# The z1 half of a gMLP input projection by a seven-product block algorithm

## The chip, the cores and the metric

The kernel runs on one NeuronCore of one Trainium2 chip. The metric is the device time of one execution in microseconds, as the median of several runs. Beside the timed runs, one further execution was recorded by the hardware profiler; all views below are of that execution.

The engines are named as the profile names them: PE is TensorE (PEld its weight loads), DVE is VectorE, ACT is ScalarE, POOL is GpSimd, SP is SyncE, which here only issues DMAs.

## The reference, cut to what matters

```python
S, D, F = 2048, 1024, 3584; Fh = F // 2            # bf16 in, bf16 out
h  = x + attention(layernorm(x))                   # 32 heads, 4 segments of 512 tokens
# the part that the change touches, with x = layernorm(h):
z  = gelu(x @ w_in)                                # w_in: 1024 x 3584
z1 = z[:, :Fh]                                     # 2048 tokens x 1792
z2 = layernorm(z[:, Fh:])
g  = w_sp @ z2 + b_sp[:, None]                     # w_sp: 2048 x 2048, over tokens
h2 = h + (z1 * g) @ w_out                          # w_out: 1792 x 1024
```

`gelu` is the tanh approximation.

## The kernel before, in words

Every operation is first recorded by a small recorder (`_Recorder.record`), which finds for each operation the earlier ones on other engines, or in DMA queues, that it has to wait for, by the memory cells that both touch. `emit` then writes each engine's operations out in the recorded order, so that all instructions carry one line in the profile, L210. The order of the program text is thus the order in each engine's own queue: an operation that waits holds up everything recorded after it on the same engine. On SP the same holds for DMA issues. SBUF regions are assigned by hand (`tens(name, shape, type, offset)`), and many are used by several tensors in turn.

The work runs in these stages, with the times of the profiled execution:

- **Attention**, to about 289 us, segment by segment, with the projections and the out-projection (`wo`) filled in between. Its last part puts the normalised activations into `HNT[s]`, four tensors of 128 x 8 x 512 bf16: for each segment s the 1024 features on partitions (eight blocks of 128) and 512 tokens along the row.
- **z2**, to 405 us: `z2_group(k, tc)` (line 798) multiplies one chunk of 128 tokens with 448 columns of `w_in`, eight matmuls into one PSUM bank, and ACT takes the bank with gelu into `Z2`. For each of four column chunks k (loaded by `win_load`, line 792, into `WIN`) it runs over 16 token chunks. `z2_stats` collects mean and variance on DVE, POOL makes the reciprocal deviation (`ZRS`), and `z2_apply` (line 822) writes the normalised chunk as fp16 into `Z2H`, on DVE, 128 x 1792. Between the groups ACT also squares the 16 row blocks of `w_sp` (`sp_norm`, line 916), because `sp_scale` (line 919) derives from the sum of squares a power of two, `SC`, with which `w_sp` is scaled to fp16.
- **z1**, to 501.5 us: the loop at line 1073 goes over four segments and 14 column blocks of 128. Each makes eight matmuls of 128 x 512, over the eight feature blocks, with the weights in `WIZ`, and ACT writes gelu into `Z1T` (features on partitions, 14 blocks, 2048 tokens). In the same stage SP loads blocks of `w_sp` transposed (`sp_load`, line 966), DVE scales them to fp16 (`sp_half`, line 971) and makes their block sums (`sp_sum`, line 974: `t1` to `t4`) and the first sums of z2 (`s_sum`, line 981, into the four parts of `SS`).
- **The gate**, `gate_group` (line 1001), in two periods (`pr`), each for 1024 output tokens. `g = w_sp @ z2` is already computed by an algorithm that cuts both factors into 2 x 2 blocks and needs seven block products instead of eight, with sums of blocks as factors (Strassen's, in Winograd's form). A group of columns has seven products (`prod`, line 991), each of eight fp16 matmuls of 128 x 512 into one bank. ACT copies the first product (`tmp_s1`), POOL adds two rows of `b_sp` (`BROW`) to it, DVE adds up the banks (`stt`), multiplies with `Z1T` in place (`out`) and makes the next group's `SS`.
- **Out**: after each period 16 units of 14 matmuls with `w_out` (`out_unit`, line 1054), added to h on DVE and stored. Next period's `w_sp` blocks are loaded and scaled meanwhile.

PSUM has eight banks, taken in rotation by `next_bank`.

Of the kernel before, what the change touches and what calls it, by code (L numbers as in the profile page):

```python
# [258 lines left out]
def bass_sequential_preLN__memory_aug_infini_attn__mixer_gmlp__prompt_kernel(  # L259
# [31 lines left out]
    class Bump:  # L291
# [4 lines left out]
        def __call__(self, name, shape, dt):  # L296
# [63 lines left out]
    WIN = [tens("win%d" % i, [128, 8, 512], BF16, o * K) for i, o in enumerate((46, 54, 190))]  # L360
    WIZ = [tens("wiz%d" % i, [128, 8, w], BF16, o * K)
           for i, (o, w) in enumerate(((54, 512), (190, 512), (118, 512), (126, 256)))]
# [3 lines left out]
    ROLES = (("b11", 46), ("b12", 22), ("b21", 198), ("b22", 14))  # L366
    RAW = {k: tens(k + "r", [128, 8, L], BF16, o * K) for k, o in ROLES}
    BH = {k: tens(k + "h", [128, 8, L], F16, o * K)
          for k, o in ROLES + (("t1", 30), ("t2", 190), ("t3", 22), ("t4", 38))}
    SS = tens("ss", [128, 4, 8, 128], F16, 54 * K)  # L370
# [3 lines left out]
    ZRS = b3("zrs", [128, NTC], F32)  # L374
    ONES = b3("ones", [128, 128], BF16)
    MHZ = b3("mhz", [128, 1], F32)
    SQ = b3("sq", [128, 16], F32)
    SQB = b3("sqb", [128, 16], BF16)
    TOT = b3("tot", [128, 1], F32)
    TOP = b3("top", [128, 1], F32)  # L380
    SC = b3("sc", [128, 1], F32)
    INV = b3("inv", [128, 1], F32)
# [3 lines left out]
    BROW = [tens("brow%d" % i, [128, L], BF16, (132 + i) * K) for i in range(2)]  # L386
    WO0 = tens("w_out0", [128, 14, 512], BF16, 118 * K)
    WO1A = tens("w_out1a", [128, 7, 512], BF16, 54 * K)
    WO1B = tens("w_out1b", [128, 7, 512], BF16, 4 * K)
    FIN = [tens("fin%d" % i, [128, 512], BF16, o * K) for i, o in enumerate((61, 11, 12, 13))]  # L390
# [26 lines left out]
    def wcols(ap, lo, hi):  # L417
        return ap[:, lo:hi].rearrange("(c p) n -> p c n", p=128)
# [371 lines left out]
    CH = [("z2", FH + 448 * k, 448) for k in range(4)] + [("z1", 512 * k, min(512, FH - 512 * k)) for k in range(4)]  # L790

    def win_load(k):
        kind, lo, w = CH[k]
        sp.dma_start((WIN[k % 3] if k < 4 else WIZ[k - 4])[:, :, 0:w], wcols(B_w_in, lo, lo + w))

    zs, zq, staged = [], [], []

    def z2_group(k, tc, stage=None):
        s, tcl = divmod(tc, 4)
        b = next_bank()  # L800
        wi = WIN[k % 3]
        mm8(PS[:, b, 0:448], lambda i: HNT[s][:, i, tcl * 128:(tcl + 1) * 128], lambda i: wi[:, i, 0:448])
        if stage is None:
            z2_gelu(k, tc, PS[:, b, 0:448])
        else:
            act.activation(ZSTG[stage][:], PS[:, b, 0:448], ACTF.Copy)
            staged.append((k, tc, ZSTG[stage][:]))
# [5 lines left out]
    def z2_stats():  # L813
        k, tc = zs.pop(0)
        dve.bn_stats(ZST[:, tc, k, :], Z2[:, tc, k * 448:(k + 1) * 448])
        if k == 3:
            dve.bn_aggr(ZMV[:, tc, :], ZST[:, tc, :, :])
            pool.tensor_single_scalar(ZRS[:, tc:tc + 1], ZMV[:, tc, 1:2], float(LN_EPS), ALU.add)
            pool.tensor_tensor(ZRS[:, tc:tc + 1], ZRS[:, tc:tc + 1], MHALF[:], ALU.pow)
            zq.append(tc)  # L820

    def z2_apply():
        tc = zq.pop(0)
        dve.tensor_scalar(Z2H[:, tc, :], Z2[:, tc, :], ZMV[:, tc, 0:1], ZRS[:, tc:tc + 1], ALU.subtract, ALU.mult)

# [93 lines left out]
    def sp_scale(b):  # L919
        pe.matmul(PS[:, b, 0:16], ONES[:], SQB[:], start=True, stop=True)  # L920
        dve.tensor_reduce(out=TOT[:], in_=PS[:, b, 0:16], axis=mybir.AxisListType.X, op=ALU.add)
        dve.tensor_single_scalar(TOT[:], TOT[:], 1e-30, ALU.max)
        pool.tensor_tensor(TOP[:], TOT[:], MHZ[:], ALU.pow)
        dve.tensor_single_scalar(TOP[:].bitcast(I32), TOP[:].bitcast(I32), 0x7F800000, ALU.bitwise_and)
        dve.tensor_single_scalar(SC[:], TOP[:], 8192.0, ALU.mult)
        dve.reciprocal(INV[:], SC[:])

# [3 lines left out]
    for it in todo:  # L931
        if isinstance(it, int):
            for half in range(2):
                wo(NSEG - 1, it, half)
                bg_pop()
            continue
        z2_group(*it)
        if it == (0, 12):
            sp_norm_load(0)
            sp_norm_load(1)  # L940
        if it[0] and it[1] > 3 or it[0] > 1:
            q = 16 * it[0] + it[1] - 20
            r = (q * 16 + 15) // 44
            if r < 16 and (q * 16 - 1) // 44 < r:
                sp_norm(r)
                if r < 14:
                    sp_norm_load(r + 2)
                elif r == 15:
                    pool.tensor_copy(SQB[:], SQ[:])
        bg_pop()  # L950
        z2_stats()
        if len(zs) > 1:
            z2_stats()
        if len(zq) > 1:
            z2_apply()
        if it == (0, NTC - 1):
            win_load(3)
        if it == (1, NTC - 1):
            for k in (4, 6, 7):
                win_load(k)  # L960
        if it == (2, NTC - 1):
            win_load(5)
# [8 lines left out]
    def sp_half(k):  # L971
        dve.tensor_single_scalar(BH[k][:], RAW[k][:], SC[:], ALU.mult)

    def sp_sum(o, a, b):
        dve.tensor_tensor(BH[o][:], BH[a][:], BH[b][:], ALU.subtract)
# [25 lines left out]
    def gate_group(pr, g, ba):  # L1001
        t1, t2 = slice(1024 * pr, 1024 * pr + 512), slice(1024 * pr + 512, 1024 * pr + 1024)
        s1, s1b1, s1b2, u2, u3 = (TMP[k][:] for k in ("s1", "s1b1", "s1b2", "u2", "u3"))
        inv = INV[:]
# [10 lines left out]
        pool.tensor_tensor(s1b1, s1, BROW[0][:], ALU.add)  # L1015
        bb, bc = next_bank(), next_bank()
# [3 lines left out]
        if pr == 0 and g == 0:  # L1020
            sp_sum("t4", "b21", "t2")
        if g < 6:
            s_sum(1, g + 1)
        prod(bb, SS[:, 2], "t3", False)
        prod(ba, a_blk(0, 1, g), "b21", False)
# [3 lines left out]
        nb = prod1(g + 1) if g < 6 else None  # L1029
        if g < 6:  # L1030
            s_sum(3, g + 1)
        stt(s1, ba, BROW[0][:])
        out(s1, 0, t1)
        prod(bc, SS[:, 3], "b22", False)
        if g < 6:
            s_sum(2, g + 1)
        prod(bb, a_blk(1, 1, g), "t4", False)
# [4 lines left out]
        stt(s1b1, bb, s1b1)  # L1042
        out(s1b1, 1, t1)
# [25 lines left out]
    for j in range(4):  # L1069
        sp_load(0, "b21", j)  # L1070
    for j in range(4):
        sp_load(0, "b11", j)
    for s in range(NSEG):
        for fc in range(14):
            k, fl = divmod(fc, 4)
            b = next_bank()
            mm8(bank(b), lambda i: WIZ[k][:, i, fl * 128:(fl + 1) * 128], lambda i: HNT[s][:, i, :])
            act.activation(Z1T[:, fc, s * 512:(s + 1) * 512], bank(b), ACTF.Gelu_apprx_tanh)
            if zq:
                z2_apply()  # L1080
            if s == 0 and fc == 6:
                sp_scale(next_bank())
            if s == 2 and fc in (6, 12):
                for k in ("b21", "b11", "b22") if fc == 6 else ("b12",):
                    sp_half(k)
            if s == 3:
                if fc == 0:
                    sp_sum("t1", "b12", "b11")
                if fc == 4:
                    s_sum(1, 0)  # L1090
                    s_sum(2, 0)
                    s_sum(3, 0)
                    s_sum(4, 0)
                if fc == 2:
                    sp_sum("t3", "b22", "b12")
                if fc == 8:
                    sp_sum("t2", "b22", "t1")
        if s == 0:
            for j in range(4):
                sp_load(0, "b22", j)  # L1100
        if s == 1:
            for j in range(4):
                sp_load(0, "b12", j)
            brow_load(0)
    sp.dma_start(WO0[:], wout[:, :, 0:512])

    units = [(tc, 0, 512) for tc in range(6)] + [(tc, 512, 512) for tc in range(8)] + [(tc, 0, 512) for tc in (6, 7)]
    nb = prod1(0)
    for g in range(7):
        nb = gate_group(0, g, nb)  # L1110
# [6 lines left out]
    act.dma_start(WO1A[:], wout[:, 0:7, 512:D])  # L1117
    act.dma_start(WO1B[:], wout[:, 7:14, 512:D])
    for n, u in enumerate(units):
        if n + 2 < 16:  # L1120
            fin_load(units[n + 2], act)
        out_unit(u, (lambda i: WO0[:, i, :]) if u[1] == 0 else
                 (lambda i: WO1A[:, i, :] if i < 7 else WO1B[:, i - 7, :]), act)
        if n == 1:
            sp_half("b11")
        if n == 4:
            sp_half("b12")
            sp_sum("t1", "b12", "b11")
        if n == 6:
            sp_half("b22")  # L1130
            sp_sum("t3", "b22", "b12")
        if n == 8:
            sp_sum("t2", "b22", "t1")
        if n == 10:
            sp_half("b21")
            sp_sum("t4", "b21", "t2")
        if n == 13:
            for k in range(1, 5):
                s_sum(k, 0)
# [9 lines left out]
    for n, u in enumerate(units):  # L1149
        if n + 2 < len(units):  # L1150
            fin_load(units[n + 2])
        tc, lo, w = u
        out_unit(u, (lambda i: WO0[:, i, 0:w]) if lo == 0 else (lambda i: Z1T[:, i, lo - 512:lo - 512 + w]))

# [29 lines left out]
```

## Time and profile before

| | us |
|---|---|
| median of three runs | 771.69 (771.63 to 772.64) |
| the profiled execution, its own time | 772.03 |
| its span, from first to last instruction | 770.3 |
| z2 stage, PE alone at work on `win` and the last `wo` | about 289 to 405.0 |
| z1 stage (`hnT,wiz` matmuls) | 405.0 to 501.5 |
| gate, first period | 501.5 to 586.4 |
| out, first period | 586.4 to 634.5 |

The page of the profile gives first the busy time of each engine and its share of the span, then the same in 40 slices, where a digit is tenths, with the clock that TensorE was granted. Section 4 is the chain of work that ended last, followed backwards from the last instruction. Section 5 groups instructions by line, engine, operation, and written and read tiles, with shapes; "x439 | 96.2, 379" reads: 439 of them, 96.2 us busy, 379 ns each. Matmuls overlap, so 379 ns is the latency of one and not its pace. The timeline shows instructions in order of time, start and length, like ones merged, and in brackets how long the engine had been idle and what ended it.

### The profile page before, as it was taken

Reading aid. Unit: us, or ns where it says so; the run is one execution under the profiler, and the core shown is the slowest. Engines: PE = TensorE matmul, PEld = TensorE weight load, DVE = VectorE, ACT = ScalarE, POOL = GpSimd, SP = SyncE. Lnnn points to the kernel's source line nnn. Section 1 sums busy time; section 2 is a strip of 40 time slices with the busy share of each in tenths; the row PEclk is TensorE's granted clock in tenths of the full one; section 3 lists DMA queues with packets and bytes.
Section 4 is the critical chain, followed back from the end, with each engine's and each line's share of the span. In section 5 each row is a group of like instructions: output and inputs, shape, how many; then the busy total and the mean of one; then the engine's idle time right before and its main releaser. Section 6 shows DMA issues by size and latency. Waiting matters only on the chain.

```text
span 770.3 us, 13128 instructions
## 1 busy us (share of the span) xinstructions
PE 761.2 (99%) x5476; PEld 367.2 (48%) x5551; DVE 464.5 (60%) x846; ACT 334.2 (43%) x395; POOL 200.0 (26%) x361
## 2 busy tenths in 40 slices
PE   8999999999999999999999999999999999999998
PEld 4445555545554545455554444444444444444444
DVE  5586589768964676754366202278785756878422
ACT  6777877777777767157783333310000000000000
POOL 2564556555653333100033000021110002112000
PEclk9999999999999999999999999999999999999999
DMA  9654555364425331765672230020019850000222
GB/s 305 168 152 89 97 83 125 83 97 84 96 57 131 84 83 37 210 173 183 198 219 55 55 67 2 1 96 1 1 34 206 229 169 7 1 1 0 62 83 75
DMA packets 133900, 75.06 MB, mean 97 GB/s; under 512 B 96208, under 2 KB 124624, under 8 KB 133840
## 3 DMA queue, kind: packets, MB, share of 16 engines
q1 hardware_dynamic: 126592, 67.40, 36.0%
q10 hardware_dynamic: 7248, 6.82, 2.8%
q8 instruction: 43, 0.70, 0.4%
q14 instruction: 17, 0.14, 0.1%
HBM read 42.74 MB, written 8.39 MB: 66 GB/s over the span
## 4 chain that ended last, share of the span: by engine, by line
PE 93%; DVE 5%; issue 1%; DMA 1%; ACT 0%; DVEq 0%
PE ps L210 93%; DVE stats L210 1%; DMA wv<-in_A_wv_dram 1%; DVE hch L210 1%; DVE otok L210 0%; DVE pqk L210 0%; DVE lno L210 0%; DVE ta L210 0%; DVE etmp L210 0%; DVE rd L210 0%; DVE rdm L210 0%; DVE mv L210 0%; ACT e L210 0%; ACT L210 0%; DVE upd L210 0%
## 5 line engine op out<-in xcount | busy, mean ns | idle before, releaser
L210 ACT ACTIVATE e<-ps 128x2048 bf16<-128x2048 f32 (+1 forms) x96 | 152.7, 1590 | 41.7 <-PE ps L210 41.5
L210 POOL TENSOR_SCALAR_AFFINE_SELECT e<-e 128x512 bf16<-128x512 bf16 x128 | 90.6, 720 | 132.4 <-ACT e L210 132.3
L210 POOL TENSOR_TENSOR tmp_s1b<-tmp_s,brow 128x512 f32<-128x512 f32 x28 | 32.3, 1155 | 255.1 <-ACT tmp_s L210 223.7
L210 PE MATMUL ps<-win,hnT 128*128 128x448 bf16 x512 | 98.3, 352 | 0.0
L210 PE MATMUL ps<-hnT,wiz 128*128 128x512 bf16 x439 | 96.2, 379 | 0.5
L210 ACT ACTIVATE tmp_s<-ps,inv 128x512 f32<-128x512 f32 x14 | 9.6, 687 | 195.1 <-DVE z1T L210 131.6
L210 PEld LDWEIGHTS ps<-win,hnT 128*128 128x128 bf16 x512 | 49.7, 98 | 46.4 <-issue 0.2
L210 PEld LDWEIGHTS ps<-hnT,wiz 128*128 128x128 bf16 x448 | 43.7, 98 | 52.7
L210 ACT ACTIVATE z1T<-ps 128x512 bf16<-128x512 f32 x56 | 33.4, 597 | 63.3 <-PE ps L210 61.1
L210 PE MATMUL ps<-xnT,wk 128*128 128x512 bf16 x233 | 59.6, 380 | 1.2
L210 PE MATMUL ps<-wv,xnT 128*128 128x512 bf16 x255 | 59.5, 380 | 0.9 <-DMA wv<-in_A_wv_dram 0.5
L210 PE MATMUL ps<-wo,oT 128*128 128x512 bf16 x254 | 57.7, 380 | 0.1
L210 DVE BATCH_NORM_STATS2 zst<-z 128x6 f32<-128x448 bf16 x64 | 38.4, 617 | 31.8 <-ACT z L210 31.3
L210 DVE TENSOR_TENSOR fin<-fin,ps 128x512 bf16<-128x512 bf16 (+2 forms) x33 | 22.1, 671 | 56.6 <-PE ps L210 48.4
L210 PE MATMUL ps<-xnT,wq 128*128 128x512 bf16 x226 | 54.0, 379 | 1.6
L210 PE MATMUL ps<-w_out,z1T 128*128 128x512 bf16 x218 | 49.3, 379 | 0.3
L210 ACT ACTIVATE z<-ps 128x448 bf16<-128x448 f32 x60 | 31.5, 541 | 37.4 <-PE ps L210 37.4
L210 PEld LDWEIGHTS ps<-v,e 128*128 128x128 bf16 x1280 | 38.8, 96 | 14.0 <-issue 6.5
L210 PE MATMUL ps<-v,e 128*128 128x33 bf16 x1280 | 42.2, 178 | 0.0
L210 DVE SCALAR_TENSOR_TENSOR tmp_u<-ps,inv,tmp_s1b 128x512 f32<-128x512 f32 x28 | 21.0, 750 | 31.3 <-PE ps L210 16.7
L210 PEld LDWEIGHTS ps<-wo,oT 128*128 128x128 bf16 x256 | 24.1, 98 | 27.6
L210 PEld LDWEIGHTS ps<-xnT,wk 128*128 128x128 bf16 x256 | 22.6, 98 | 29.9 <-issue 5.0
(137 smaller groups left out, 1101.0 us busy)
## 6 DMA issues: line engine op xcount, KB each, us to landing
sj<-in_B_w_sp_dram SPq DMA_DIRECT2D x16, 512.0 KB, 3.5
xch<-in_A_x_dram SPq DMA_DIRECT2D x16, 256.0 KB, 3.6
xr<-in_A_x_dram SPq DMA_DIRECT2D x16, 256.0 KB, 4.0
out_dram<-hch SPq DMA_DIRECT2D x16, 256.0 KB, 2.4
win<-in_B_w_in_dram SPq DMA_DIRECT2D x4, 896.0 KB, 5.3
wiz<-in_B_w_in_dram SPq DMA_DIRECT2D x3, 1024.0 KB, 6.2
wo<-in_A_wo_dram SPq DMA_DIRECT2D x1, 2048.0 KB, 8.7
fin<-out_dram ACTq DMA_DIRECT2D x16, 128.0 KB, 3.4
```

The source lines that it names most:

```text
L210: ins = getattr(e, op.name)(*op.args, **op.kw)
```

## The change

z1 is computed by the same seven-product algorithm as the gate. Both factors are cut in two along the features (blocks 0 to 3 and 4 to 7) and, respectively, along the columns (first and second 896) and along the tokens (segments 2p and 2p + 1). A group is now one column block of each half and two segments: 7 groups in each of two periods p, 14 in all, of seven products of four matmuls.

- The weights' z1 half is loaded in column pairs (`WZ`, 2 x 256 columns; the last 2 x 128), scaled in place to fp16 (`WZH`) by a power of two from their largest magnitude (`wz_norm`, DVE; `scale_of`, one matmul on PE in the z2 stage), and the gelu's `scale` takes the power back (`INV[1]`).
- Four sums of weight blocks per group (`sz_sum`, 128 x 512 fp16) are made on POOL, four sums of activations per period (`hn_sum`, in halves of 128 x 1024) on DVE.
- In a group ACT copies the first product, DVE adds banks (five operations of 128 x 512), ACT writes four gelus. The products of successive groups are interleaved by the table `offs`.
- `z2_apply` leaves the z2 stage: eight run on DVE and eight on ACT, in z1's first eight groups.
- The fp16 scaling of the first period's `w_sp` blocks moves from DVE to ACT, in quarters (`sp_part`), in z1's groups 8, 9, 10 and 12; their transposed loads move to z1's second half.
- `t1`, `t2` and the first `SS` follow after z1's last step on DVE; `t3` and `t4` are made in the first gate group, half on POOL and half on DVE, in quarters. Ahead of that PE gets the first two products of groups 0 and 1 (`pre`). `brow_load` follows after z1, and `BROW[1]` takes the region of one of the weight sums.
- In `gate_group` the order of some operations changes.
- The squares of `w_sp` are spread over 37 groups of z2 instead of 44, and many regions move.

The core of the diff:

```diff
+    def wz_load(q):
+        w = 256 if q < 3 else 128
+        for i in range(2):
+            lo = 896 * i + 256 * q
+            sp.dma_start(WZ[q][:, :, i, :], wcols(B_w_in, lo, lo + w))
...
+    def hn_sum(p, t, h, eng=dve):
+        a, b = {1: (hb(0, 1, p), hb(0, 0, p)), 2: (hb(1, 1, p), HT[p][1][:]),
+                3: (hb(1, 1, p), hb(0, 1, p)), 4: (hb(1, 0, p), HT[p][2][:])}[t]
+        s = slice(2 * h, 2 * h + 2)
+        eng.tensor_tensor(HT[p][t][:, s, :], a[:, s, :], b[:, s, :], ALU.subtract)
...
+    for r in range(16):
+        q = (37 * r + 15) // 16
+        at(q, sp_norm, r)
+        if r < 14:
+            at(q, sp_norm_load, r + 2)
+    at(37, pool.tensor_copy, SQB[:], SQ[:])
+    for k in range(12):
+        at(k + 1, wz_norm, (1, 2, 0)[k // 4], k % 4)
+    for k in range(8):
+        at(3 + 2 * k, hn_sum, 0, (1, 2, 3, 4)[k // 2], k % 2)
+    at(18, wz_norm, 3, 0)
+    at(19, wz_norm, 3, 1)
+    at(20, pool.tensor_copy, SQB[:, 0:14], SQZ[:])
+    at(25, scale_of, 1, 14, None)
+    for k in range(8):
+        at(26 + k, wz_half, k // 2, k % 2)
...
-        if len(zq) > 1:
+        if len(zq) > 16:
             z2_apply()
         if it == (0, NTC - 1):
+            for k in (1, 2, 0):
+                wz_load(k)
             win_load(3)
...
-    for s in range(NSEG):
-        for fc in range(14):
-            k, fl = divmod(fc, 4)
-            b = next_bank()
-            mm8(bank(b), lambda i: WIZ[k][:, i, fl * 128:(fl + 1) * 128], lambda i: HNT[s][:, i, :])
-            act.activation(Z1T[:, fc, s * 512:(s + 1) * 512], bank(b), ACTF.Gelu_apprx_tanh)
...
+    def z1_step(g, k):
...
+        for i in range(4):
+            pe.matmul(b, ka[:, i, :], kb[:, i, :], start=(first and i == 0), stop=(i == 3), skip_group_check=True)
+        if k == 1:
+            act.activation(s1, b, ACTF.Copy)
+        if k == 6:
+            dve.tensor_tensor(u2, b, s1, ALU.add)
+        if k == 5 and g < 13:
+            for x in (1, 2):
+                sz_sum(g + 1, x)
+        if k == 7:
+            dve.tensor_tensor(u3, b, s1, ALU.add)
+            dve.tensor_tensor(u3, bank(zb[g, 2]), u3, ALU.add)
+            z1_out(fc + 7, 2 * p + 1, u3)
+            if g < 13:
+                sz_sum(g + 1, 3)
+        if k == 2:
+            z1_out(fc, 2 * p, b)
...
+        if k == 4:
+            dve.tensor_tensor(s1, b, s1, ALU.add)
+            z1_out(fc + 7, 2 * p, s1)
+        if k == 3:
+            dve.tensor_tensor(u2, b, u2, ALU.add)
+            z1_out(fc, 2 * p + 1, u2)
+            if g < 12:
+                sz_sum(g + 2, 4)
...
+    for g in range(8):
+        on(g, 6, lambda: zq and z2_apply())
+        on(g, 4, lambda: zq and z2_apply(True))
+    for k in range(8):
+        on((0, 1, 2, 3, 4, 4, 5, 5)[k], 3 if k < 5 else (7, 3, 7)[k - 5], hn_sum, 1, (1, 2, 3, 4)[k // 2], k % 2)
+    on(1, 7, scale_of, 0, 16, None)
+    for k, g, r in (("b11", 6, 3), ("b12", 6, 3), ("b22", 8, 3), ("b21", 10, 3)):
+        for j in range(4):
+            on(g, r, sp_load, 0, k, j)
+    for n, (k, g) in enumerate((("b11", 8), ("b12", 9), ("b22", 10), ("b21", 12))):
+        for r in range(4):
+            on(g, (6, 7, 2, 4)[r], sp_part, k, r)
+    offs = {1: -5, 6: 0, 5: 1, 7: 3, 2: 4, 4: 6, 3: 12}
+    for x, g, k in sorted((7 * g + offs[k], g, k) for g in range(14) for k in offs):
+        z1_step(g, k)
+    for k in ("t1", "t2"):
+        for r in range(4):
+            sp_sum(k, r)
+    for k in range(1, 5):
+        s_sum(k, 0)
+    brow_load(0)
+    for i in range(2):
+        sp.dma_start(WO0[i][:], wout[:, 7 * i:7 * i + 7, 0:512])
...
-    nb = prod1(0)
-    for g in range(7):
+    pre = [(prod1(g), prod2(g)) for g in range(2)]
+    nb2 = gate_group(0, 0, *pre[0])
+    nb = gate_group(0, 1, *pre[1])
+    gate_group(0, 2, nb2, nx=False)
+    for g in range(3, 7):
         nb = gate_group(0, g, nb)
```

And in `gate_group`:

```diff
+        if pr == 0 and g == 0:
+            for r in range(4):
+                sp_sum("t3", r, pool if r < 2 else dve)
         bb, bc = next_bank(), next_bank()
         prod(bb, SS[:, 1], "t2", True)
         prod(bc, SS[:, 0], "t1", True)
         stt(u2, bb, s1b2)
         if pr == 0 and g == 0:
-            sp_sum("t4", "b21", "t2")
+            for r in range(4):
+                sp_sum("t4", r, pool if r < 2 else dve)
+        nb = prod1(g + 1) if bd is None and g < 6 and nx else None
         if g < 6:
             s_sum(1, g + 1)
+            s_sum(2, g + 1)
         prod(bb, SS[:, 2], "t3", False)
-        prod(ba, a_blk(0, 1, g), "b21", False)
+        if bd is None:
+            prod(ba, a_blk(0, 1, g), "b21", False)
+        elif nx:
+            nb = prod1(g + 2)
         stt(u3, bb, s1b2)
```

## The prediction, made before the changed kernel had run

> **What bounds the kernel now.** I read the page's busy shares first, then the chain that ended last, then the timeline of TensorE by stage.
>
> ```profile
> PE 761.2 (99%) x5476; PEld 367.2 (48%) x5551; DVE 464.5 (60%) x846; ACT 334.2 (43%) x395; POOL 200.0 (26%) x361
> PEclk9999999999999999999999999999999999999999
> PE 93%; DVE 5%; issue 1%; DMA 1%; ACT 0%; DVEq 0%
> ```
>
> TensorE is busy 99%, carries 93% of the chain and is at full clock in all 40 slices. From 289 to 768 us the chain is PE with gaps of 0.05 us. Time therefore falls only by removing matmuls, and any wait that newly reaches PE is paid in full. Since PE never waits there, none of the waits costed below can come out under zero.
>
> ```profile
> 405.00 7.29 PE L210 MATMUL ps<-hnT,wiz 128*128 128x512 bf16 x33
> ...
> 501.50 1.89 PE L210 MATMUL ps<-b11h,z2h 128*128 128x512 f16 x8
> 503.23 1.89 PE L210 MATMUL ps<-t2h,ss 128*128 128x512 f16 x8
> ```
>
> z1 runs from 405.00 to 501.50 us: 448 matmuls, 0.2154 us each from start to start. An fp16 product of eight takes 503.23 - 501.50 = 1.73 us, 0.216 each: both types cost the same. (The rows' 379 ns is the latency of one, not its pace.)
>
> **What the change removes.** z1 has 14 groups of 7 products of 4 matmuls: 392 instead of 448. 56 x 0.2154 = **-12.1 us**. The scale of the weights adds one matmul (0.17 us). fp16 weights against bf16 activations are in no row; since bf16 with bf16 and fp16 with fp16 agree, I take no difference. One step of four is 0.863 us, one group of seven 6.05 us. The gate still has 2 x 7 groups of seven products: no gain there.
>
> **The z2 stage (289 to 405 us): 0, from 0 to 3.** A group of 8 is 1.51 us on PE, and PE needs only ACT to empty its banks, eight in rotation. ACT gets the same 16 squares (1.90 + 0.19 us) in 37 groups instead of 44: per group 0.54 + 2.09 x 16/37 = 1.44 of 1.51 us. On SP, six weight loads (3.1 MB) now stand ahead of the third square's row. The windows at 8 to 12 us, 512-byte runs, show some 290 GB/s, so 10.8 us, plus 2.8 for `win3`, 1.5 for the row and 1 to be seen; four of the loads can start at about 335 (data from 336.4), since their regions are free. The row lands near 352.5, and the square wants it at 347.7: ACT stalls 5 us, with the gelus queued behind it. Before, such a wait stood here, and PE ran on:
>
> ```profile
> 373.06 1.91 ACT L210 ACTIVATE sj<-sj 128x2048 bf16<-128x2048 bf16 x1 [3.86 <-DMA sj<-in_B_w_sp_dram]
> ```
>
> Eight banks cover 12 us less the square and a gelu; the row would have to come 4 us later to reach PE. DVE loses 14 applies of 0.74 and gets 14 maxima (1.2 us, by the 685 ns reduce of 512), 8 differences (0.69) and 8 scalings (0.68). The weights' scale then needs its maxima before PE reaches that matmul, queued in front of all later groups, at 377.5 us. DVE's statistics wait for ACT's delayed gelu until 355.6; then come 8 maxima x 1.13, 6 differences x 0.61 and 12 statistics x 0.55 in pace, 19.3: ready at 375, 2 us to spare. Both margins used up and a little more: 3.
>
> **The z1 stage: +2, from 0 to 5.** Per group, on DVE: five sums with a bank, 5 x 0.69 (`tm<-ps,rdm`) = 3.5; an apply, 0.75, in groups 0 to 7; about one half of a difference, 0.69, in groups 1 to 6. 4.9 of 6.05. On ACT: one copy and four gelus, 3.0 in pace, plus an apply of 1.8, or four scalings of 1.06 (groups 8, 9, 10 and 12): 7.1 against 6.05. ACT falls behind by 1.1 in three groups running, but the copy that it delays is wanted four steps later, and I count 0.6 us left at the tightest. So 0, up to 2 if the scalings are longer or a transposed block lands late: before, b12's four transposes took 8.05 us from issue (453.35) to use (461.40), and the last block, b21, has 9.6 between the product that frees its region and ACT's turn. Behind these transposes SP has only `brow` and WO0, wanted at the gate and 80 us later. On POOL: four weight sums of 128x512 f16, which no row shows. The two-input POOL row is `tmp_s1b` f32, 1155 ns; the one-input `e` in bf16 takes 640 to 720. Take 1.155, since two 16-bit inputs resemble the first: 4.6, plus 0.25.
>
> Each engine fits alone. What does not is DVE and POOL together:
>
> ```profile
> 135.36 0.42 DVE L210 TENSOR_SCALAR etmp<-etmp 128x1024 bf16<-128x1024 bf16 x1
> 135.82 1.00 DVE L210 TENSOR_TENSOR pqk<-pqk,etmp 128x1024 bf16<-128x1024 bf16 x1
> 135.40 0.87 POOL L210 TENSOR_SCALAR_AFFINE_SELECT e<-e 128x512 bf16<-128x512 bf16 x1
> ```
> ```profile
> 514.67 1.20 DVE L210 TENSOR_TENSOR z1T<-tmp_u,z1T 128x512 bf16<-128x512 f32 x1
> 514.17 1.15 POOL L210 TENSOR_TENSOR tmp_s1b<-tmp_s,brow 128x512 f32<-128x512 f32 x1 [7.71 <-ACT tmp_s L210]
> ```
> ```profile
> 491.34 2.29 DVE L210 TENSOR_TENSOR t2h<-b22h,t1h 128x4096 f16<-128x4096 f16 x1 [5.58 <-remote]
> 506.05 2.56 DVE L210 TENSOR_TENSOR t4h<-b21h,t2h 128x4096 f16<-128x4096 f16 x1
> 504.19 2.27 POOL L210 TENSOR_TENSOR tmp_s1b<-tmp_s,brow 128x512 f32<-128x512 f32 x2 [79.52 <-ACT tmp_s L210]
> ```
>
> At 135 us POOL waits for DVE's `etmp` to end (135.78), then DVE's next waits until POOL ends (136.27): they alternate. At 514 a DVE product of two SBUF tensors takes 1.20 instead of 0.69, ending 0.55 after POOL. The last pair is a block sum in f16: 2.29 alone, 2.56 where POOL overlaps its start. In contrast the DVE operation before it, one input in PSUM, ran at 0.75 under POOL. The Trainium skill ("SBUF — State Buffer", Who interferes with whom) gives the rule: a DVE instruction with two SBUF inputs and a GpSimd instruction that reads SBUF exclude each other for their whole length. Read the other way, that engines with queues of their own overlap freely, the gate's term below would be 0.4 us; by the rule it is 11.
>
> In z1 only differences and applies are caught. The chain from product 3 to the next product 7 is u2 0.7, difference 0.6, s1 0.7, u2 0.7 and a 0.2 semaphore, 2.9 of the 3.45 that four steps give; a wait of up to 1.0 for POOL puts 0 to 0.5 on PE, over 8 differences and the double ones in groups 4 and 5: 2 us. With no waits 0; with every one full, 5.
>
> **The start of the gate: +11.3, from 0.4 to 12.** Before, `t1`, `t3`, `t2` and the first four `ss` ran in z1's idle DVE (477 to 494 us), POOL idle. Now t1, t2 and ss stand behind z1's last DVE operation, and half of t3 and t4 goes to POOL. Let z1 end at 0. PE has four products that need none of it, 6.9 us, then `t2` and `t1`, so it wants `t3` at 10.4. DVE owes, before the sum `u2` that frees t3's bank: z1's last u2 (to 0.9), then eight quarter sums, four ss, two quarters of t3, 14 x 0.6 (687 ns in pace) = 8.4. Alone: 9.3, and u2 to 10.1: a stall near 0.4 for the wait of the first product on ss. But POOL starts at about 3, when `brow` has landed (its region is read by z1's last matmul), with two sums of 1.02 holding the port and four quarters of 128x1024 f16, twice the elements: 1.9 each, 9.6 in all. All 14 DVE operations read two SBUF tensors, at least nine remain, and the two alternate. So 0.9 + 8.4 + 9.6 = 18.9, u2 to 19.7: PE waits 9.4. Groups 1 and 2 run six products (10.4) against DVE's 9.7 and a wait for POOL's next pair: 1.2 and 0.7 more. Sum 11.3. If POOL's f16 quarters took half as long, 7.5.
>
> The gate's later groups hold seven products (12.1) against DVE's 9.7 (six sums from a bank at 0.77 in pace, four products and four ss at 0.6 to 0.65), and the reordered s_sum and z1T products stay covered. WO0, WO1 and the second period's transposes keep their places on SP and ACT.
>
> **The sum.** PE's products -12.1, the scale's matmul 0.2, z2 0, z1's port 2, z1's ACT 0, gate 11.3: -12.1 + 0.2 + 0 + 2 + 0 + 11.3 = +1.4 us. Against the profiled execution: span 770.3, its own time 772.03 (1.7 around the span), so 773.4. The median of the runs is 0.34 below that execution: 773.1. What this kernel's measurement can tell from no change is about 0.2%, 1.5 us.
>
> **Rivals.**
> - *The port costs little*: POOL's f16 is short, or DVE slips several operations in. Then gate 0.4, z1 1: -12.1 + 0.2 + 1.4 = -10.5, or **761.2**. For it: 60% DVE and 26% POOL, each with room. Against it: the alternation above.
> - *POOL bounds z1 (slower)*: place, the four weight sums of a group. With d for one, POOL needs 4d + 0.25 + about 1.2 of waits in groups 1 to 7, so it decides from d = 1.15, and in groups 8 to 13 from 1.45. At d = 1.5: 7 x 1.4 = 9.8, less 2.4 of lead, +7.4 over the sum, and 2.8 more at the gate: **783**. For it: 1.155 is already that point. Against it: 16-bit POOL rows are shorter than f32 ones, not longer.
> - *The matmuls don't fall*, as when fp16 with bf16 ran slower: each 1% on 392 matmuls is 0.8 us, so at 14% the whole gain is gone, and with the waits above it ends near **785**. No row suggests it, and I leave it no chance of its own.
>
> The Trainium skill ("ScalarE: Activation LUTs", Table sets) says that identity is in every set, so the new applies on ACT should load no table; no row here shows Identity. With a table load each way (1283 ns in this trace) they would put ACT at 4.8 + 2.6 = 7.4 of 6.05.
>
> **How the numbers follow.** Forecast, gain given back at the gate: 0.6; its own range 767 to 778 (gate 7.5 to 12, z1 0 to 5, z2 0 to 3), so faster 0.2, same 0.17, slower 0.23 of it. Port cheap, 0.2: faster. POOL-bound, 0.2: slower. Together 0.40, 0.17, 0.43. For 8 in 10, 763 to 780.
>
> **What would show it.** Right: 392 matmuls in z1 in 84 to 90 us; after them four fp16 products and then PE idle 4 to 10 us, ended by DVE ss and by tmp_u; DVE's quarter sums there above 1 us each, alternating with POOL. Wrong: PE dense across that seam (rival one); PE waiting on POOL sz inside z1 (rival two), or on the scale near 377 us (my z2 term).

## The result, and the profile after

The changed kernel takes 774.97 us (median of four runs, 774.80 to 775.99), against 771.78 us for the kernel before on the same chip (four runs, 771.63 to 772.64): a ratio of 1.0042, 95% interval [1.0024, 1.0059]. It is slower by 3.2 us. The profiled execution took 774.8 us, with a span of 773.1.

Of the page, these are the busy times, TensorE's busy tenths and granted clock in 40 slices, and the engines' shares of the chain that ended last:

```profile
PE 758.1 (98%) x5496; PEld 361.7 (47%) x5496; DVE 551.2 (71%) x956; ACT 373.4 (48%) x433; POOL 292.6 (38%) x430
PE   9999999999999999999999999969999999999998
PEclk9999999999999999999999999989999999999999
PE 82%; DVE 7%; ACT 4%; POOL 2%; issue 2%; DMA 2%; POOLq 0%; ACTq 0%; DVEq 0%
```

DVE is busy for 87 us more than before and POOL for 93 more; an operation that is held up by the other engine counts as busy, so part of both is waiting. TensorE's share of the chain fell from 93% to 82%: waits reach it now. One slice, from 502.5 to 521.8 us, shows where: busy 6 tenths, and a clock below full.

TensorE's timeline at the seam from z1 to the gate (start, length, operation; in brackets the idle time before it and what ended it):

```profile
490.80 1.89 PE L210 MATMUL ps<-b11h,z2h 128*128 128x512 f16 x8
...
498.72 1.90 PE L210 MATMUL ps<-t2h,ss 128*128 128x512 f16 x8 [0.85 <-DVE ss L210]
500.46 1.89 PE L210 MATMUL ps<-t1h,ss 128*128 128x512 f16 x8
508.51 3.60 PE L210 MATMUL ps<-t3h,ss 128*128 128x512 f16 x8 [6.17 <-DVE tmp_u L210]
511.90 3.04 PE L210 MATMUL ps<-b11h,z2h 128*128 128x512 f16 x8
```

z1 ends at 490.80. It lasted from 404.29, 86.5 us, where it took 96.5 before. The four products that need nothing of DVE follow (the first row and the three left out behind it), then `t2` waits for `ss`, and `t3` for u2 (`tmp_u`). The row of `t3` and the next are 3.60 and 3.04 long instead of 1.89: their first 14 matmuls start 0.43 us apart instead of 0.216, half speed.

What DVE and POOL did meanwhile (same columns):

```profile
491.61 2.48 DVE L210 TENSOR_TENSOR t1h<-b12h,b11h 128x1024 f16<-128x1024 f16 x4
494.01 2.49 DVE L210 TENSOR_TENSOR t2h<-b22h,t1h 128x1024 f16<-128x1024 f16 x4
496.42 0.68 DVE L210 TENSOR_TENSOR ss<-z2h 128x1024 f16<-128x1024 f16 x1
497.14 1.53 DVE L210 TENSOR_TENSOR ss<-ss,z2h 128x1024 f16<-128x1024 f16 x1
498.59 1.64 DVE L210 TENSOR_TENSOR ss<-z2h 128x1024 f16<-128x1024 f16 x1
500.15 2.60 DVE L210 TENSOR_TENSOR ss<-z2h,ss 128x1024 f16<-128x1024 f16 x1
502.68 5.12 DVE L210 TENSOR_TENSOR t3h<-b22h,b12h 128x1024 f16<-128x1024 f16 x2
507.72 0.74 DVE L210 SCALAR_TENSOR_TENSOR tmp_u<-ps,inv,tmp_s1b 128x512 f32<-128x512 f32 x1
```
```profile
496.25 3.42 POOL L210 TENSOR_TENSOR tmp_s1b<-tmp_s,brow 128x512 f32<-128x512 f32 x2 [11.05 <-DMA brow<-in_B_b_sp_dram]
499.64 5.08 POOL L210 TENSOR_TENSOR t3h<-b22h,b12h 128x1024 f16<-128x1024 f16 x2
504.69 5.08 POOL L210 TENSOR_TENSOR t4h<-b21h,t2h 128x1024 f16<-128x1024 f16 x2
```

Until POOL gets in, a DVE quarter takes 0.6 us in pace (2.48 for four). From the second `ss` (497.14) on, a DVE sum takes some 1.6 beside a sum of 128x512 and 2.60 beside a quarter of 128x1024, and POOL's quarters take 2.54 each: one of either, in turn.

The account of the span from z1's start on, all by start-to-start gaps of the two traces: z1's products -12.1, z1's waits +1.9, start of the gate +11.5 (`t2` 1.0, `t3` 6.3, half speed 2.8, `t3` of groups 1 and 2 0.3 and 1.05), and `t3` of group 6 in both periods 2 x 1.05. Together +3.4; z1 started 0.7 earlier (405.00 to 404.29, the scale's matmul included), so 2.7, where the spans differ by 2.8.

### The profile page after: what moved, and what is told of

The parts are those of the page before. It is cut to its first block, busy times and chain, and to the rows that moved or that the text cites. A ratio compares the mean times of both kernels' runs of the same rounds, so it can differ in the third digit from the quotient of the medians.

```text
span 773.1 us, 13378 instructions
## 1 busy us (share of the span) xinstructions
PE 758.1 (98%) x5496; PEld 361.7 (47%) x5496; DVE 551.2 (71%) x956; ACT 373.4 (48%) x433; POOL 292.6 (38%) x430
## 4 chain that ended last, share of the span: by engine, by line
PE 82%; DVE 7%; ACT 4%; POOL 2%; issue 2%; DMA 2%; POOLq 0%; ACTq 0%; DVEq 0%
PE ps L210 82%; ACT sj L210 3%; DMA sj<-in_B_w_sp_dram 2%; DVE ss L210 2%; DVE tmp_u L210 1%; ACT z L210 1%; DVE z1T L210 1%; POOL zrs L210 1%; POOL sz L210 1%; DVE t3h L210 1%; DVE zt L210 1%; DVE tmp_s1b L210 0%; DVE t2h L210 0%; DVE t1h L210 0%; DVE ht L210 0%
## 5 line engine op out<-in xcount | busy, mean ns | idle before, releaser
L210 POOL TENSOR_TENSOR tmp_s1b<-tmp_s,brow 128x512 f32<-128x512 f32 x28 | 42.8, 1546 | 175.8 <-ACT tmp_s L210 164.1
L210 PE MATMUL ps<-w_out,z1T 128*128 128x512 bf16 x336 | 74.0, 379 | 0.0
L210 DVE TENSOR_TENSOR zt<-ps,zt 128x512 f32<-128x512 f32 x70 | 47.7, 688 | 20.6 <-PE ps L210 17.3
L210 PE MATMUL ps<-xnT,wq 128*128 128x512 bf16 x256 | 60.5, 379 | 0.0
L210 PEld LDWEIGHTS ps<-w_out,z1T 128*128 128x128 bf16 x336 | 32.9, 98 | 39.6
L210 DVE RECIPROCAL rd<-ps 128x16 f32<-128x16 f32 x32 | 8.0, 250 | 47.1 <-PE ps L210 46.9
L210 PE MATMUL ps<-t3h,ss 128*128 128x512 f16 x112 | 28.2, 397 | 9.0 <-DVE tmp_u L210 9.0
```

The lines of the kernel that those rows point to most:

```text
L210: ins = getattr(e, op.name)(*op.args, **op.kw)
```

## The experiments

Each kernel is the changed kernel with the edit shown. Ratios are to the kernel before, run on the same chip; "against the change" is the difference to 1.0042, times 772 us. As a second yardstick, the seam is the time from z1's end to the start of `t3` in group 2, in the profiled execution: 42.6 us in the changed kernel (490.80 to 533.43).

**All quarters on DVE.**

```
-                sp_sum("t3", r, pool if r < 2 else dve)
+                sp_sum("t3", r, dve)
...  (t4 alike)
```

> All eight quarters of t3 and t4 are made on DVE, none on POOL. Theory (DVE and POOL take the shared SBUF port in turns): POOL holds the port for its two sums with brow only, 2.0 us, so DVE ends its 16 operations ahead of u2 at 490.8 + 0.9 + 16 x 0.6 + 2.0 + 0.7 = 504.0 instead of 508.5; TensorE's wait before t3 falls from 6.3 us to about 2, the half-speed matmuls behind it (3.0 us) go away; 775.0 falls to 766 to 770. Rival (DVE simply has too many operations behind z1, whatever POOL does): two more of them ahead of u2 make the wait 1.2 us longer, 775 to 777.

Measured: 772.0 us, ratio 0.9995 [0.9987, 1.0004], 3.6 us less than the change. The direction is the port's, and the rival's (a longer wait) is excluded. The size is about half of what I expected. TensorE at the seam:

```profile
506.86 1.90 PE L210 MATMUL ps<-t3h,ss 128*128 128x512 f16 x8 [1.61 <-DVE tmp_u L210]
508.59 1.89 PE L210 MATMUL ps<-b11h,z2h 128*128 128x512 f16 x8
511.25 1.90 PE L210 MATMUL ps<-t4h,z2h 128*128 128x512 f16 x8 [0.77 <-DVE tmp_u L210]
...
519.92 1.90 PE L210 MATMUL ps<-t3h,ss 128*128 128x512 f16 x8 [1.59 <-DVE tmp_u L210]
```

The wait before `t3` is down to 1.8 us and nothing runs at half speed, as expected. But `t4` and the `t3` of group 1 now wait for u2 and u3, which stand behind DVE's longer queue: 2.7 us where the changed kernel had 0.3. The seam is 37.7 us, 5.0 shorter. In this execution z1 was 1.6 us longer (below) and began 1.3 later, which takes part of it back.

**POOL loaded without a reader.** To the kernel with all quarters on DVE, eight POOL sums are added that nobody waits for.

```
+        if pr == 0 and g == 0:
+            for r in range(8):
+                pool.tensor_tensor(DMY[:], BH["b22"][:, r, :], BH["b21"][:, r, :], ALU.subtract)
```

> As in the kernel with all quarters of t3 and t4 on DVE, but POOL makes eight sums of 128x512 f16 behind its two with brow, the port time of the four quarters that it had; nothing reads their result. Theory (the port: DVE gives way to POOL, whoever needs POOL's result): DVE's operations ahead of u2 lengthen by about one POOL operation each, the wait before t3 goes back up by 3 to 5 us and the half-speed matmuls return, 774.5 to 776. Rival (TensorE waited for POOL's quarters as such, their length and their late start): with no reader of POOL's results nothing changes, 771.5 to 772.5.

Measured: 778.45 us, ratio 1.0083 [1.0068, 1.0098]. Against the kernel without these sums that is 0.0088, or 6.8 us, for work that no engine waits for. DVE's own four quarters of `t3`, and the wait:

```profile
503.28 6.30 DVE L210 TENSOR_TENSOR t3h<-b22h,b12h 128x1024 f16<-128x1024 f16 x4
```
```profile
510.30 3.60 PE L210 MATMUL ps<-t3h,ss 128*128 128x512 f16 x8 [6.38 <-DVE tmp_u L210]
```

Four quarters take 6.30 us instead of 2.49. This shows the port as such: DVE's sums and POOL's take turns, one for one, whoever reads POOL's results. The seam is 44.6 us, 7.0 longer than without these sums, so the loss lies there. The wait before `t3` rose by 4.8 us (1.8 to 6.5 by the gaps), inside the 3 to 5 expected; the half speed came back with 2.5, `t4` and `t3` of group 1 still wait 2.4, and I had counted on more of that being hidden.

**`brow` early.** Its rows go to a region that is free sooner and are loaded in z1's last group.

```
+    on(13, 4, brow_load, 0)
...
-    brow_load(0)
```

> The two brow rows are loaded in z1's last group, to a region that is free by then, so that POOL can start when ACT's copy is there, at about 493.5 instead of 496.2. Theory (port taken in turns): POOL's six operations only take the port from DVE's earlier sums instead of the later ones; remaining 11 x 0.6 of DVE and up to 9.6 of POOL end at 507.5 to 510.4, so t3's wait stays or grows by up to 2 us: 775 to 777. Rival (the late landing of brow is what delays t3, POOL's quarters being the last thing awaited): everything comes 2.7 us earlier, and with it part of the half-speed stretch: 770 to 772.3.

Measured: 779.72 us, ratio 1.0093 [1.0078, 1.0107], 3.9 us more than the change; seam 44.8, so 2.2 of it at the seam; z1 was 1.7 longer in the profile (its start, below). An earlier start of POOL is a loss, so `brow`'s late landing was no cause of the waits. It was a shelter. The theory's sign was right and its size too small, because I had the six POOL operations delay u2 alone. They now fall on the quarters of `t2` and on `ss`, which the first of the two products needs:

```profile
510.56 3.59 PE L210 MATMUL ps<-t2h,ss 128*128 128x512 f16 x8 [9.49 <-DVE ss L210]
```

**DVE's sums early.** `t1` and the four `ss` are made in z1's last group; POOL keeps its quarters.

```
+    for k in range(1, 5):
+        on(13, 2, s_sum, k, 0)
+    for r in range(4):
+        on(13, 4, sp_sum, "t1", r)
...  (and both go from behind z1's last step)
```

> The four sums ss of group 0 and the four quarters of t1 are made inside z1's last group, where DVE has idle time; only t2 and the shared t3 and t4 stay behind z1. POOL's quarters stay. Theory (what makes TensorE wait is DVE's queue behind z1, each entry of which gives way once to POOL): six operations are left ahead of u2, t2's wait of 1.0 us goes, t3 waits only for POOL's own quarters (5.4 for brow, 2 x 1.02, 2 x 2.05 = 11.6 us after z1's end against 10.4 wanted), 1 to 2 us instead of 6.3, no half-speed matmuls; group 1 then shows a lag of 1 to 2 us, as when the quarters were DVE's: 7 us less, 767 to 770. Rival (TensorE waits for POOL, the last holder of the port, and DVE's amount does not matter): the wait before t3 stays at 5 us or more, 773 to 776.

Measured: 774.08 us, ratio 1.0024 [1.0015, 1.0034], 1.4 us less than the change; seam 39.9. Here the rival comes nearer: 4.6 us of wait where it had 5 or more, and a time within its 773 to 776.

```profile
506.50 0.59 PE L210 MATMUL ps<-t3h,ss 128*128 128x512 f16 x2 [2.77 <-POOL t3h L210]
508.93 2.74 PE L210 MATMUL ps<-t3h,ss 128*128 128x512 f16 x6 [1.84 <-POOL t3h L210]
```

`t2` waits no more, but `t3` waits 4.6 us for POOL's own quarters. Their turns are lengthened by DVE, which is at `t4` and the next `ss` by then, and they began late: POOL's first sum needs ACT's copy, which stood behind z1's last gelu, and that behind DVE's last sum of z1, now later; then DVE's own quarters kept it out for 2.2 us more. So both queues count, as users of one port. Removing DVE's entries alone or moving POOL's forward (the experiment before) only changes which of the two is late.

**The order of products without cover.** In the groups with no other product between `t1` and `t3` (2, and 6 twice) the product with `b21` goes ahead of `t3`.

```
+        late = bd is None and (g == 6 or not nx)
+        if late:
+            prod(ba, a_blk(0, 1, g), "b21", False)
         prod(bb, SS[:, 2], "t3", False)
...  (and not behind it in these groups)
```

> In the groups with no product of a later group between t1 and t3 (group 2 of the first period, group 6 of both) the product with b21 is put ahead of t3. Theory (the three waits of 1.05 us before t3 come from the order of the products alone): they vanish, -3.1 us, 771.9. Rival (DVE is behind in these groups, and any order meets its lag): the wait moves to the next product, 775.

Measured: 776.15 us, ratio 1.0051 [1.0039, 1.0063]: no gain. The rival was right, in detail:

```profile
582.33 1.89 PE L210 MATMUL ps<-t3h,ss 128*128 128x512 f16 x8
585.07 1.90 PE L210 MATMUL ps<-t4h,z2h 128*128 128x512 f16 x8 [0.85 <-DVE tmp_u L210]
```

`t4` goes to the same bank as `t3`, after u3 has read it. With `b21` taken away from between them, the same 1.0 us stands before `t4`.

**The fourth `ss` later.** In the changed kernel this is what DVE does at the seam of two groups:

```profile
578.76 1.64 DVE L210 TENSOR_TENSOR ss<-z2h,ss 128x1024 f16<-128x1024 f16 x1
580.32 0.74 DVE L210 SCALAR_TENSOR_TENSOR tmp_u<-ps,inv,tmp_s1b 128x512 f32<-128x512 f32 x1
```
```profile
576.68 3.17 POOL L210 TENSOR_TENSOR tmp_s1b<-tmp_s,brow 128x512 f32<-128x512 f32 x2 [8.92 <-ACT tmp_s L210]
```
```profile
581.12 1.90 PE L210 MATMUL ps<-t3h,ss 128*128 128x512 f16 x8 [0.89 <-DVE tmp_u L210]
```

In the kernel before, at the same seam, the fourth `ss` stood two operations further ahead of u2 and ran at full speed, and `t3` did not wait:

```profile
575.72 0.68 DVE L210 TENSOR_TENSOR ss<-z2h,ss 128x1024 f16<-128x1024 f16 x1
...
577.74 0.75 DVE L210 SCALAR_TENSOR_TENSOR tmp_u<-ps,inv,tmp_s1b 128x512 f32<-128x512 f32 x1
```
```profile
579.20 1.89 PE L210 MATMUL ps<-t3h,ss 128*128 128x512 f16 x8
```

In the changed kernel u2, which `t3` waits for, is queued directly behind a sum that POOL holds up and that only the group's last product needs. The edit queues it behind u2.

```
         stt(u2, bb, s1b2)
+        if g:
+            s_sum(4, g)
...
         out(u2, 0, t2)
-        if g < 6:
-            s_sum(4, g + 1)
```

> The fourth sum ss of the next group, the last DVE operation of each gate group, is made in the next group behind u2 (its product is the group's last). Theory (the waits of 1.05 us before t3 in groups 2, 6 and 6 come from this sum, which POOL's two sums hold from 0.69 to 1.64 us, and behind which u2 is queued): these waits go, -2 to -3 us against the changed kernel, about 772. Rival (u2 waits for POOL's sum with brow itself): the waits stay, 775.

Measured: 771.61 us, ratio 0.9995 [0.9986, 1.0004], 3.6 us less than the change. TensorE's waits from z1 to the second period's end:

```profile
PE ps L210 <- DVE tmp_u L210: 6.2, 1, 6.2
PE ps L210 <- DVE zt L210: 0.9, 2, 0.6
PE ps L210 <- DVE ss L210: 0.9, 1, 0.9
```

In the changed kernel the first of these rows read:

```profile
PE ps L210 <- DVE tmp_u L210: 9.0, 5, 6.2
```

(total, times, longest). Of the five waits one is left, the first group's; the waits of groups 1, 2, 6 and 6, 3.5 us by their gaps, are gone. A cause in the order of DVE's queue is thereby shown.

**z1's start.** Loads and the end of the scale are moved.

```
-            for k in (1, 2, 0):
+            for k in (1, 2):
                 wz_load(k)
-            win_load(3)
...
+    at(1, wz_load, 0)
+    at(8, win_load, 3)
...
+    on(3, 7, scale_end, 0)     # the last three operations of scale_of(0)
```

> Two edits at z1's start: the loads of the first weight pair and of the last z2 chunk stand behind the rows that ACT squares, and the end of the scale of w_sp (three small DVE operations that wait for POOL's power) is queued two groups later. Theory (the waits in z1 come from work that spills over from z2, and from this scale): the 0.9 us at 420 goes in every execution, and the 1.8 us at 410 to 413 that three of five profiles show goes too: -1 to -2.7 us, 773 to 774.5. Rival (DVE's port waits on the differences and applies make them, whatever stands around them): the waits move to the next products, 775 to 776.

Measured: 774.42 us, ratio 1.0026 [1.0017, 1.0036], 1.2 us less than the change. z1 took 85.3 us instead of 86.5 (TensorE at 404.48 to 489.76), with waits of 0.1 and 0.5 us left. The two edits were not run apart. In the changed kernel DVE's timeline shows what the wait at 420 came from:

```profile
415.65 0.15 DVE L210 TENSOR_SCALAR tot<-tot 128x1 f32<-128x1 f32 x1
417.24 0.15 DVE L210 TENSOR_SCALAR top<-top 128x1 int32<-128x1 int32 x1 [1.44 <-POOL top L210]
```

An operation of 0.15 us holds DVE for 1.44 us, because POOL's power of one column is queued behind a sum of weight blocks. The other wait, 0.7 to 1.9 us at 409 to 413, shows in five of the nine profiled executions with the changed kernel's order of loads (the changed kernel, seven of its variants and the second filler run), though not in the changed kernel's own. Here it is with all quarters on DVE:

```profile
413.33 1.90 PE L210 MATMUL ps<-z1x,sz 128*128 128x512 f16 x8 [0.55 <-POOL sz L210]
```

In that execution ACT's third square, which waits for its row behind the weight loads, came 0.7 us later than in the changed kernel (from the z2 stage's start), and POOL's first weight sum, behind the reciprocal deviations that follow from ACT's gelus, 1.9 us later. None of the three profiles with the moved loads shows the wait; with five of nine against none of three this is likely the cause, not proved.

**A filler in the wait.** 28 matmuls without use stand between `t1` and `t3` of the first group.

```
+        if pr == 0 and g == 0:
+            for i in range(28):
+                pe.matmul(bank(...), a_blk(0, 0, 0)[:, i % 8, :], BH["b11"][:, i % 8, :], start=True, stop=True)
         prod(bb, SS[:, 2], "t3", False)
```

> 28 further matmuls, whose result is not used, stand between t1 and t3 of the first gate group, 28 x 0.216 = 6.0 us in a wait of 6.3. Theory (after an idle stretch of some 6 us TensorE runs 14 matmuls at half speed, and that is a cost by itself): the 0.43 us steps go back to 0.216 and 3.0 us are gained with the same DVE and POOL work, 772.0. Rival (these matmuls are slow because DVE and POOL hold the memory they read): the 0.43 us steps stay behind t3, 775 or a little more.

Measured: 776.0 us, ratio 1.0041 [1.0028, 1.0054], no gain. Its profiled execution, at 781.27 us, was no typical one: POOL got to the port among the quarters of `t2`, and not only at the second `ss` as in the changed kernel's, so that the long wait (5.65 us) stood before `t2` and the filler came on top. This profile does not tell the two apart; a second one of the same kernel does.

> The kernel with 28 further matmuls once more, for a profile of an execution in which the wait lies behind t1. Theory (the half-speed stretch costs 3.0 us by itself): t3 and the product behind it run at 0.216 us each, and TensorE is 3.0 us earlier at the end of group 2. Rival (DVE's lag stands right behind it, so the matmuls' speed does not matter): the stretch is at full speed, but t4 of group 0 or t3 of group 1 then wait 2 to 3 us more than the 0.3 of the changed kernel.

Measured: 774.93 us in one run, full clock throughout.

```profile
509.01 1.90 PE L210 MATMUL ps<-t3h,ss 128*128 128x512 f16 x8
510.75 1.89 PE L210 MATMUL ps<-b11h,z2h 128*128 128x512 f16 x8
513.47 1.90 PE L210 MATMUL ps<-t4h,z2h 128*128 128x512 f16 x8 [0.83 <-DVE tmp_u L210]
...
522.15 1.90 PE L210 MATMUL ps<-t3h,ss 128*128 128x512 f16 x8 [1.59 <-DVE tmp_u L210]
```

`t3` and its successor run at full speed, so the half speed did come from the idle time. But the 2.8 us that the half speed had cost are not earned: `t4` and group 1's `t3` wait 2.7 us where they had waited 0.3. The seam is 42.3 us, 0.35 shorter. The slow matmuls had covered DVE's lag. The kernel with z1's start moved shows the same without a filler: in its profile only 7 matmuls were slow, group 1's `t3` waited 1.4 us, and the seam is 42.3 too.

**All together.** Quarters on DVE, early sums, the late fourth `ss` and z1's start in one kernel.

> All that helped together: quarters of t3 and t4 on DVE, early sums, the late fourth sum, and the two edits at z1's start. Theory (the seam's waits are DVE's queue and the port, and nothing else stands behind them): at the start of the gate DVE owes 8 x 0.6 + 2.0 of POOL, u2 is ready at 8.4 us against 10.4 wanted, so no wait before t2 and t3; of the 15.3 us of waits at most 1 to 3 are left: 761 to 764. Rival (TensorE meets the next wait at once, since DVE's own load in groups 1 and 2 binds): 766 to 769.

Measured: 763.7 us, ratio 0.9894 [0.9879, 0.9909]: 1.1% faster than the kernel before and 11.4 us below the change. The four edits alone sum to 9.9. Seam 33.9. The busy line, the chain and the waits left:

```profile
PE 750.0 (99%) x5422; PEld 361.1 (47%) x5496; DVE 536.2 (70%) x960; ACT 374.9 (49%) x433; POOL 285.6 (38%) x426
PE 91%; DVE 6%; issue 1%; DMA 1%; POOL 1%; ACT 0%; ACTq 0%; DVEq 0%
```
```profile
501.46 1.90 PE L210 MATMUL ps<-t3h,ss 128*128 128x512 f16 x8 [1.04 <-DVE tmp_u L210]
506.13 1.90 PE L210 MATMUL ps<-t4h,z2h 128*128 128x512 f16 x8 [1.04 <-DVE tmp_u L210]
513.37 1.90 PE L210 MATMUL ps<-t3h,ss 128*128 128x512 f16 x8 [0.16 <-DVE tmp_u L210]
```

**Two edits more:** `brow` early, and in the first group `ss` 1 and 2 of the next behind u3.

> The kernel with all edits together, with two more: brow is loaded in z1's last group, and in the first gate group the sums ss 1 and 2 of the next group are queued behind u3. Theory (in the kernel with all edits the two waits of 1.2 us before t3 and t4 come from u2 waiting for POOL's sum with brow, which landed late and was then held off by DVE, and from u3 queued behind six DVE operations): both go, -2 us, 761 to 762. Rival (with POOL in earlier, DVE's t2 and t3 quarters alternate with it and are late in turn, as when brow alone was early): the same or up to 2 us more, 763.5 to 766.

Measured: 763.75 us, ratio 0.9893 [0.9876, 0.9909], seam 33.9: the same. The wait before `t4` went, and group 1's `t3` waits 1.5 us instead of 0.3. `brow`'s early landing did nothing, since POOL's first sum waited for ACT's copy here and began 6.3 us after z1's end in both kernels. So the rival had the number right and not its reason (POOL in earlier). The wait before `t3` is 1.2 us in both: u2 waits for that sum, which DVE's back-to-back sums keep out until 9.7 us after z1. The other wait only moved from `t4` to the next group: what TensorE meets there is DVE's own queue.

## Why the prediction was right, and where it was not

The forecast was slower by 1.4 us with the mechanism "gain given back at the gate"; it was 3.2, and the gain went there.

- **PE's products, -12.1.** As forecast: z1's 392 matmuls keep 0.863 us per step of four, mixed types too.
- **z2, 0 from 0 to 3.** In the profile it was 0: ACT stalled for the row 6.0 us (5 forecast) and the scale did not hold PE. But the slack was as thin as the bound said: in five of nine executions a wait stands at z1's start, likely this delay.
- **z1, +2 from 0 to 5.** Measured 1.9. The size was right and the place partly wrong. I had charged the port waits of differences and applies; 0.9 of it came from the scale of `w_sp`, whose one-column operation waits for POOL. I had listed POOL's 0.25 for small operations, but not who is queued behind the answer. The eight applies on ACT, 1.87 us each, brought no table load: both traces show two, the last near 300 us.
- **The gate's start, +11.3.** Measured 11.5, and the load experiment shows its mechanism. The steps inside were off. I let POOL start 3 us after z1 and u2 be ready at 19.7; POOL started at 5.4, `brow` having taken 5.1 us, and held DVE up only from 6.3 on; u2 ended 17.7 after z1 (508.46), five of six POOL operations before it. PE's wait was 7.3, not 9.4. A part of it, 1.0, fell on `t2`, for which I had only the 0.4 of the case without POOL. Half speed after the wait, 2.8, was not foreseen. Groups 1 and 2 waited 0.3 and 1.05 (1.2 and 0.7 forecast). That the total came out was luck in part, yet not all: the filler shows that DVE's lag sets the end of this stretch, with slow matmuls or without.
- **"Gate's later groups ... stay covered", 0.** This step failed, and it is about the difference between forecast and result: 2.1 us in group 6 of both periods. I compared DVE's load per group (9.7) with TensorE's (12.1). What counts is the order. Before, only `t1` stood between `t2` and `t3` in every group, and none waited. The change put the fourth `ss` at the end of a group's queue on DVE, directly ahead of the next u2, where POOL's two sums hold it for 1.64 us instead of 0.68. `b11`'s product of the next group, moved ahead of `t3`, covers this; a group without a next one has no such cover. With the `ss` behind u2 these waits were gone.
- **The rivals.** "The port costs little" is excluded by the 6.8 us of the load experiment; its time, 761, is not far from the 763.7 of the kernel with all edits, which takes POOL's quarters out of the seam. "POOL bounds z1" did not occur: a weight sum takes 1.15 us, as taken, and POOL was late only at z1's start.

## What to carry to other kernels

Where DVE's operations have two SBUF inputs and POOL reads SBUF beside them, moving work from one to the other hides nothing: cost each sum twice, once on each queue, and count instructions as well as microseconds. In z1, where most of DVE's sums have one input in PSUM, 70 us of POOL's work left TensorE with 1.9 us of waits. When a product order is changed, check for every group, first and last above all, what stands between two products of one bank, and what is queued on the adding engine ahead of the sum that frees it. A saving in one stage is kept only if the work that used that stage's idle engines still has a place.

## What the runs showed of the hardware

- **Taking turns has an entry.** Back-to-back DVE sums, each begun before the last one's end, kept POOL out in most executions: its first sum took 1.86 us in the changed kernel, 2.86 with the quarters on DVE and 4.41 with all edits, always 1.0 us beyond the first point where DVE's next operation depended on its last or was not there. In two profiled executions (`brow` early, the first filler) it got in at the next operation. After that they alternate without exception while both have work: a pair takes 1.56 us with a POOL sum of 128x512 f16 (POOL load, start to start) and 2.52 with a quarter of 128x1024, of which DVE's part is its 0.6. The Trainium skill ("SBUF — State Buffer", Who interferes with whom) says that whoever issues first holds the port for the whole instruction and that issue order decides who blocks. The alternation agrees with the first; the entry does not fit the second: with all edits, five DVE sums that began after POOL's ran ahead of it. What decides the entry these runs leave open.
- **The clock after a wait.** After 6.2 us without a matmul 14 ran at 0.43 us each in the changed kernel, but only 7 in the kernels with the other order of products and with z1's start moved; over the seven profiles with a wait of 5.7 to 9.5 us it was 7 to 14. After waits up to 1.8 us (kernel with all quarters on DVE) none did, and the granted clock was 1.000. The Trainium skill ("TensorE: Matmul & The Clock Gate", Part 1) gives a window of some 3.4 us of idleness, and half speed after it; these observations agree with it. The kernel with DVE's sums early does not plainly: there waits of 2.8 and 1.8 us, with two matmuls between, were followed by 7 slow matmuls.
- **The landing of a small load varies, and here it mattered little.** The 128 KB rows of `brow` landed 3.1 to 5.2 us after issue over all runs; the row at the seam took 5.1 in the changed kernel's profile and 4.0 to 4.3 in the nine others with the same order of issues. Yet in the seven profiles where POOL's first sum was ready 4.4 to 5.5 us after z1's end, it ended 7.3 us after it in every one, because DVE's back-to-back sums kept it out. Only in the first filler's, ready at 4.3, did it get in sooner, which moved the long wait from `t3` to `t2`.
